# A fused attention and phase-MLP kernel: a fixed order of instructions in place of a scheduler, with gated loads, another way for one batch's transposes, and zero products in TensorE's gaps

## The chip, the cores and the metric

The kernel runs on one core of one Trainium2 chip. The metric is the device time of one execution in microseconds (us). All inputs lie in HBM as float32; q, k, v and the weights are turned into bf16 while they are loaded, and the output is float32.

Names used below: TensorE (PE in the profile; PEld is its weight load), VectorE (DVE), ScalarE (ACT), GpSimd (POOL), SyncE (SP). "Software loads" are DMAs that POOL issues; "hardware loads" are DMAs that SP or ACT issue.

## The reference

Four batches of 768 positions go through sparse attention (8 heads of 64), then through a layer that mixes positions and channels. Cut to what matters:

```python
# attention: keep the first 8 keys and a band of 96 keys behind each query
scores = (q @ k^T) / sqrt(64) - slope[h] * dist(i, j)     # masked where not kept
x = softmax(scores) @ v                                    # to (batch, 768, 512)
# the second layer
theta = x @ w_theta
y = w_tok_r @ (x * cos(theta)) + w_tok_i @ (x * sin(theta))   # mixes the 768 positions
u = x + y
out = u + relu(u @ w_ch)
```

Within a batch everything before the mixing is local to a third of the positions (256). The mixing needs x of the whole batch. So each batch passes through scores, exponentials, values, transposes of x, theta, cosine and sine, mix, u, transposes of u, and the channel product. Other batches' work can fill TensorE while one batch waits.

## The kernel before

The kernel builds a list of named operations with guessed durations, then a list scheduler in Python chooses at build time, greedily by earliest start, the order in which they are written out. Each engine then gets its own instructions in that order, and one that has to wait holds up those behind it.

```python
class Plan:
    LAT = 0.2
    ...
    def schedule(self):
        ...
        while ready:
            best = None
            for o in ready:
                for e, dur in o.eng.items():
                    ...
                    s = max(t, free.get(e, 0.0))
                    key = (s if len(o.eng) == 1 else s + dur * 0.0, o.prio)
                    if best is None or key < best[0]:
                        best = (key, o, e, s, dur)
        ...
        return sorted(order, key=lambda o: o.start)
```

All loads are issued by POOL, one after the other; the code sets no limit on how many are under way. The trace shows one all the same: the loads take turns at eight semaphores that tell of their landing, never more than eight were under way at once, and 26 were issued within 0.45 us of the landing of the load eight places before. There are 80 loads; most bring 128 positions of q, k or v (128 KB once they are bf16):

```python
def load(fn, nbytes, ndesc, reads=(), writes=(), alloc=None):
    nload[0] += 1
    add(f"load{nload[0]}", {"POOL": 0.62 + 0.00028 * ndesc}, fn, ...,
        after=[f"load{nload[0] - 1}"] if nload[0] > 1 else [])
```

From batch 1 on, two small jobs are done by hardware DMAs on SP's queue, beside the loads: the copy of v whose first 8 rows are the global keys (vp), and the transposes of x (and of u):

```python
def vprev(b, g, prio):
    ...
    if b == 0:
        ...   # two copies on DVE
    else:
        add(f"vpa{b}{g}", {"SP": 0.5}, lambda: nc.sync.dma_start(out=dst[NG:T], in_=src[NG:T]), ...)
        add(f"vpb{b}{g}", {"SP": 0.5}, ...)          # the first 8 rows, by DMA too

def xtrans(b, g, prio):
    if b == 0:
        ...   # eight transposes on TensorE, then an evacuation by DVE or ACT
    else:
        add(f"xt{b}{g}", {"SP": 0.5},
            lambda: nc.sync.dma_start_transpose(out=new(xt, "xT", [T, NP, 2, T], BF)..., in_=tiles[xk]...), ...)
```

The keys are kept twice, side by side (one copy gets the global keys). One instruction reads the transposed k from PSUM and writes both copies:

```python
kk = new(dst, "kk", [T, NP, 2, 2, T], BF)
vector[o.took](out=kk.rearrange("d p t r n -> d (p t) r n"),
               in_=tiles[ps].rearrange(...)[:, :, None, :].to_broadcast([T, 2 * NP, 2, T]))
```

PSUM is cut into two tiles of two banks ("big": scores, theta, values in pairs) and four of one bank ("small"). Before its first data arrive TensorE runs eight products of zeros.

The softmax here doesn't subtract the row's maximum and nothing guards it: scores larger than these inputs give would overflow.

## Time and profile before

| | before |
|---|---|
| median time, us | 202.90 (4 runs, 202.41 to 203.18) |
| span of the profiled run, us | 200.8 |
| busy: PE, DVE, ACT, POOL, us | 168.4, 124.7, 92.4, 69.4 |
| granted TensorE clock, mean over the span | 0.937 |
| first theta product, us | 29.12 |
| TensorE waiting for xT, us | 16.7 |

The page cuts the span into 40 slices; each digit is the busy share in tenths, and the PEclk row is the granted clock in tenths. The view of windows gives, for a stretch, the busy time of PE, PEld, DVE, ACT and POOL with the number of instructions in brackets, then the clock, the DMA share and GB/s. The list of waits gives who waited for what: microseconds in all, times, and the longest. The lines of these views are in the prediction below.

```profile
67.52 1.52 SPq L481 DMA_TRANSPOSE xT<-x  x1
...
81.70 0.87 SPq L373 DMA_DIRECT2D vp<-vn  x1
...
83.53 1.51 SPq L481 DMA_TRANSPOSE xT<-x  x1
```

SP stood for 80.5 us in all in front of copies of v whose v had not landed, and what was to be sent later waited behind them. This is a good part of the hole. The x of batch 1's second third was ready at 69.6 us, but in the scheduler's order two copies of batch 2's v come before its transpose; their v landed at 72.65 and 81.64 us, so the transpose left SP at 83.53, 13.9 us late, and landed at 92.99. The transpose of the first third (x ready at 62.5 us) had left at 67.52 and landed at 77.21: 5.1 us in SP's queue and 9.7 in transit.

### The profile page before, as it was taken

To read this page: it belongs to the slowest core of one execution; us is meant where nothing else is said; L and a number is where in the kernel's file an instruction comes from. 1 tells how busy PE (TensorE), PEld (TensorE's weight loads), DVE (VectorE), ACT (ScalarE), POOL (GpSimd) and SP (SyncE) were. 2 spreads that over 40 slices of the span, in tenths; PEclk is the share of its full clock that TensorE was granted. 3 is DMA by queue.
4 is the path that set the end of the run, shared out by engine and by line. 5 is a ranking of instruction groups with operands and counts; after the bars stand their busy time and mean duration, and the time that the engine had idled before them with its cause. 6 is when DMAs were issued, how large, how long until landed. Compare 5 with 4: busy or idle time off the path is not lost.

```text
span 200.8 us, 3765 instructions
## 1 busy us (share of the span) xinstructions
PE 168.4 (84%) x1532; PEld 88.5 (44%) x1532; DVE 124.7 (62%) x243; ACT 92.4 (46%) x100; POOL 69.4 (35%) x85
## 2 busy tenths in 40 slices
PE   7589999899589906804999799999999998999982
PEld 2355466555245502401364355547454653444430
DVE  5475994958496920700397788677988775634351
ACT  2038758899355400600487464187764609400010
POOL 7999745479686855720072000000000000000000
PEclk9859999999999975965899999999999999999998
DMA  5999999999999999999799442832114466124432
GB/s 37 133 147 152 187 210 208 176 154 161 152 184 182 185 138 199 145 148 201 118 102 169 91 131 66 177 100 65 54 30 106 103 148 116 52 52 140 126 104 104
DMA packets 101224, 26.37 MB, mean 131 GB/s; under 512 B 94351, under 2 KB 97055, under 8 KB 101207
## 3 DMA queue, kind: packets, MB, share of 16 engines
q0 software_dynamic: 77568, 12.85, 90.5%
q1 hardware_dynamic: 23639, 13.28, 28.9%
q8 instruction: 12, 0.20, 0.4%
q14 instruction: 5, 0.04, 0.1%
HBM read 25.69 MB, written 6.29 MB: 159 GB/s over the span
## 4 chain that ended last, share of the span: by engine, by line
PE 47%; DMA 33%; POOL 10%; DVE 4%; issue 2%; ACT 1%; SPq 1%; POOLq 0%
PE ps L534 24%; DMA qk<-in_k_dram 11%; PE ps L573 8%; DMA xT<-x 7%; POOL qk L256 6%; PE pb L492 5%; DMA w_nat<-in_moe_w_tok_i_dram 5%; DMA vn<-in_v_dram 5%; DMA out_dram<-o 4%; POOL vn L269 4%; PE pb L448 3%; PE pb L401 3%; DMA uT<-u 2%; PE ps L338 2%; DVE kk L348 1%
## 5 line engine op out<-in xcount | busy, mean ns | idle before, releaser
L534 PE MATMUL ps<-zri,w_tokT 128*128 128x512 bf16 x288 | 70.3, 381 | 0.4 <-ACT w_tokT L327 0.4
L418 ACT ACTIVATE e<-pb 128x1024 bf16<-128x1024 f32 (+1 forms) x48 | 43.9, 951 | 36.3 <-PE pb L401 36.0
L492 PE MATMUL pb<-w_theta_bf,xT 128*128 128x512 bf16 x96 | 25.7, 416 | 16.7 <-DMA xT<-x 16.7
L534 PEld LDWEIGHTS <-w_tokT 128*128 128x128 bf16 x288 | 26.2, 98 | 28.7 <-issue 1.4
L545 DVE TENSOR_TENSOR u<-x,ps 128x512 bf16<-128x512 bf16 x24 | 16.4, 685 | 32.3 <-PE ps L534 32.2
L256 POOL DMA_DIRECT2D qk<-in_q_dram x24 | 21.3, 894 | 25.7 <-PE ps L338 14.7
L426 DVE TENSOR_TENSOR e<-e,etab 128x1024 bf16<-128x1024 bf16 (+1 forms) x36 | 23.0, 642 | 6.7 <-ACT e L418 6.4
L573 PE MATMUL ps<-w_ch_bf,uT 128*128 128x512 bf16 x96 | 24.7, 379 | 1.8 <-DMA uT<-u 1.1
L256 POOL DMA_DIRECT2D qk<-in_k_dram x24 | 21.2, 892 | 5.7 <-DMA qk<-in_q_dram 2.3
L269 POOL DMA_DIRECT2D vn<-in_v_dram x24 | 21.2, 907 | 5.5 <-DMA qk<-in_k_dram 2.0
L492 PEld LDWEIGHTS <-xT 128*128 128x128 bf16 x96 | 9.5, 105 | 30.1 <-DMA xT<-x 18.3
L580 DVE SCALAR_TENSOR_TENSOR o<-ps,u 128x512 f32<-128x512 f32 x24 | 16.6, 690 | 10.0 <-PE ps L573 9.8
L505 ACT ACTIVATE cs<-pb,halfpi 128x1024 bf16<-128x1024 f32 x12 | 13.4, 1114 | 17.5 <-PE pb L492 17.4
L513 DVE TENSOR_TENSOR zri<-x,cs 128x1024 bf16<-128x1024 bf16 x24 | 16.3, 686 | 5.3 <-ACT cs L505 4.8
L338 PE MATMUL ps<-ident,qk 128*128 128x128 bf16 x192 | 15.6, 230 | 4.7 <-DMA qk<-in_q_dram 2.4
L348 DVE COPY kk<-ps 128x2048 bf16<-128x2048 bf16 x12 | 14.5, 1220 | 4.9 <-PE ps L338 4.9
L401 PE MATMUL pb<-qT,kk 64*128 64x128 bf16 x352 | 17.0, 223 | 0.4 <-DVE rec L460 0.4
L401 PEld LDWEIGHTS <-kk 64*128 64x128 bf16 x352 | 10.2, 96 | 14.4 <-issue 12.0
L338 PEld LDWEIGHTS <-qk 128*128 128x128 bf16 x192 | 12.4, 102 | 8.7 <-DMA qk<-in_q_dram 3.4
L505 ACT ACT_TABLE_LOAD x4 | 5.1, 1283 | 23.5 <-PE pb L492 23.5
L448 PEld LDWEIGHTS <-e 128*128 128x128 bf16 x352 | 13.3, 97 | 5.2 <-issue 1.4
L573 PEld LDWEIGHTS <-uT 128*128 128x128 bf16 x96 | 8.5, 98 | 10.8 <-DMA uT<-u 1.7
(53 smaller groups left out, 146.7 us busy)
## 6 DMA issues: line engine op xcount, KB each, us to landing
out_dram<-o SPq DMA_DIRECT2D x24, 256.0 KB, 2.3
qk<-in_q_dram POOLq DMA_DIRECT2D x24, 128.0 KB, 8.3
qk<-in_k_dram POOLq DMA_DIRECT2D x24, 128.0 KB, 8.3
vn<-in_v_dram POOLq DMA_DIRECT2D x24, 128.0 KB, 8.4
vp<-vn SPq DMA_DIRECT2D x9, 243.8 KB, 8.2
w_nat<-in_moe_w_tok_r_dram POOLq DMA_DIRECT2D x3, 384.0 KB, 11.0
w_nat<-in_moe_w_tok_i_dram POOLq DMA_DIRECT2D x3, 384.0 KB, 11.7
w_theta_bf<-in_moe_w_theta_dram POOLq DMA_DIRECT2D x1, 512.0 KB, 6.9
```

Source lines behind the costliest of these rows:

```text
L256: nc.gpsimd.dma_start(out=tiles["qk", b, g][:, i, t].rearrange("p (h d) -> p h d", d=D), in_=(q, k)[i][b, :, r0:r0 + T, :].rearrange("h p ...
L269: nc.gpsimd.dma_start(out=v_bufs[i][:, t, :, 0:D], in_=v[b, :, r0:r0 + T, :].rearrange("h p d -> p h d"))
L338: nc.tensor.transpose(p_[:, p, t * T:(t + 1) * T], src[:, i, t, p * T:(p + 1) * T], ident)
L401: nc.tensor.matmul(p_[:, hh, s * T:(s + 1) * T], lhsT=tiles["kk", b, kg][R, p, kt, r, :], rhs=tiles["qT", b, g][R, p, qt * T:(qt + 1) * T] ...
L418: nc.scalar.activation(e_[:, :, 0:n], tiles[pb][:, :, 0:n * T].rearrange("p a (s n) -> p a s n", n=T), AF.Exp, scale=scale)
L426: nc.vector.tensor_mul(e_[:, :, 0:n], e_[:, :, 0:n], etab[:, 2 * p:2 * p + 2, s0:s0 + n])
L448: nc.tensor.matmul(o, lhsT=l_, rhs=r_, start=(i == 0), stop=(i == len(mms) - 1))
L492: nc.tensor.matmul(p_[:, t, :], lhsT=tiles["xT", b, g][:, p, t, :], rhs=w_theta_bf[:, p, :], start=(p == 0), stop=(p == NP - 1))
L505: nc.scalar.activation(c_[:, 0], tiles[pb], AF.Sin, bias=halfpi)
L534: nc.tensor.matmul(p_, lhsT=w_tokT[wi][:, 2 * g + t, tt * T:(tt + 1) * T], rhs=tiles["z", b, g][:, wi, t, :], start=(g == 0 and t == 0 and ...
L573: nc.tensor.matmul(p_, lhsT=tiles["uT", b, tt][:, p, :], rhs=w_ch_bf[:, p, :], start=(p == 0), stop=(p == NP - 1))
L580: nc.vector.scalar_tensor_tensor(o_, in0=tiles[ps], scalar=0.0, in1=tiles[uk], op0=ALU.max, op1=ALU.add)
```

## The change

The scheduler is taken out, and a list of some 940 names fixes the order. A name may carry the engine that does it ("/DVE") and a number of zero products to put ahead of it ("+27"). With it come changes of method. In the words of the change's title: gated loads; the first third of q and k by hardware loads; the second copy of k from SBUF; zero products in TensorE's gaps; forced table loads. In the diff there is more: x of batch 1 is transposed on TensorE, all vp copies are on DVE, all PSUM tiles are of one bank, and the loads come in another order (the token weights in twelve loads rather than six, between the others). The core of the diff, with cuts:

```diff
-    def schedule(self):
-        ...
+    def issue(self, order):
+        for n in order:
+            n, _, pad = n.partition("+")
+            n, _, eng = n.partition("/")
+            op = self.ops[n]
+            op.took, self.pad = eng or op.took, int(pad or 0)
+            op.fn()
+
+ORDER = """
+ones6 hw00 hw10 zero rel ones3 tiny hw01 halfpi hw11 warm0 ... t0001+27 load8 cast11/DVE ...
+... gate20 x0210 xc01/DVE bi0221+1 load20 v020 x0211 s022 n020 tw00 gate21 ... ch351 o35 st34 o351 st35 st351
+"""
-    bufs = dict(qk=5, ..., cs=2, ..., w_nat=6, big=2, small=4)
+    bufs = dict(qk=6, ..., cs=3, ..., w_nat=7, pa=4, pb=4)      # pa, pb: one PSUM bank each
+    def fill(p_, acc=False):
+        for _ in range(plan.pad):
+            ...  nc.tensor.matmul(p_, lhsT=zero[:, 0:T], rhs=zero[:, 0:p_.shape[-1]], start=not acc, stop=not acc)
-    NV = 6
+    NV = 7
+    VP_ENG = (1, 1, 1, 1)     # copies of v on DVE in all batches
+    X_PE = (1, 1, 0, 0)       # x transposed on TensorE in batches 0 and 1
+    U_PE = (1, 0, 0, 0)
+    DEPTH = 5
+    DP = 80                   # v padded from 65 to 80 columns a head
     ...
+        if depth:
+            add(f"gate{n}", {"POOL": 0.35},
+                lambda: nc.gpsimd.tensor_copy(out=scrap, in_=landed[n - depth]()),   # reads one element of load n-5
+                reads=[("ld", n - depth)], ...)
     ...
+    def first(i, t):          # first q/k third: float32 by hardware load, then a cast
+            (nc.sync, nc.scalar)[i].dma_start(out=a, in_=(q, k)[i][0, :, t * T:(t + 1) * T, :]...)
     ...
+            def copy():       # second copy of k: from SBUF
+                vector[oc.took](out=d_[:, :, :, 1, NG:T], in_=d_[:, :, :, 0, NG:T])
     ...
+            add(f"tx{b}", {"ACT": 1.36}, lambda: nc.scalar.activation(tiny, tiny, AF.Exp), ...)
+        add(f"ts{b}", {"ACT": 1.36}, lambda: nc.scalar.activation(tiny, tiny, AF.Sin), ...)
```

A gate is a POOL copy of a single element that load number n-5 has brought; as POOL works in order, load n is not issued before load n-5 has landed (for every load from 20 on, the first that is gated). So the gates bring loads under way down to five. A forced table load is an activation of one element that makes ScalarE load the table of Exp or Sin at a moment when it is free.

## The prediction

> **What bounds the kernel now.** I read the page first (engine shares, the 40 slices), then the windows cut at the points where the character of the 40 slices changes, then the waits of TensorE, the timeline of TensorE in the worst stretch, and the two tiles that travel by hardware DMA.
>
> The page, shares and slices:
>
> ```profile
> PE 168.4 (84%) x1532; PEld 88.5 (44%) x1532; DVE 124.7 (62%) x243; ACT 92.4 (46%) x100; POOL 69.4 (35%) x85
> ...
> PE   7589999899589906804999799999999998999982
> ...
> PEclk9859999999999975965899999999999999999998
> DMA  5999999999999999999799442832114466124432
> ```
>
> TensorE is the bound from slice 20 on (9s to the end), but slices 13 to 19 hold a hole with the clock down to 5 or 6 tenths, and the first slices are half empty. Each slice is 5.02 us. The DMA row is 9 for the first 19 slices and falls to 1 to 6 afterwards: the hole in TensorE ends where the load queue runs dry. The same, by stretches:
>
> ```profile
> 7.00:29.00 22.00, 19.55 (x267) 12.04 (x265) 15.86 (x39) 11.47 (x13) 18.29 (x24) 0.84 1.89 168
> 29.00:60.00 31.00, 26.67 (x266) 15.98 (x265) 22.25 (x41) 23.56 (x30) 21.34 (x25) 1.00 2.09 174
> 60.00:69.80 9.80, 9.80 (x132) 5.37 (x129) 7.67 (x16) 5.46 (x6) 7.25 (x10) 1.00 2.14 182
> 69.80:101.90 32.10, 15.94 (x94) 7.22 (x91) 9.09 (x17) 7.12 (x7) 11.76 (x14) 0.73 1.82 158
> 101.90:162.00 60.10, 58.50 (x603) 31.20 (x602) 47.96 (x85) 35.59 (x38) 4.85 (x6) 1.00 0.55 99
> ```
>
> After the window and its length come PE, weight loads, DVE, ACT and POOL busy, the granted clock, DMA share and GB/s. From 69.80 to 101.90 only 94 matmuls ran in 32.10 us, at a mean clock of 0.73; the next 60.10 us ran 603 at 58.50 busy. What TensorE waited for:
>
> ```profile
> PE pb L492 <- DMA xT<-x: 16.7, 4, 8.4
> PE ps L338 <- DMA qk<-in_q_dram: 2.4, 3, 1.5
> PE ps L338 <- DMA qk<-in_k_dram: 1.7, 4, 0.6
> PE pb L393 <- DVE dtab L232: 1.6, 1, 1.6
> ```
>
> L492 is the theta product; it waits for the attention output of batch 1, transposed by a hardware DMA. Its timeline lines, and the landing times of the two tiles that go by DMA transpose:
>
> ```profile
> 77.26 3.20 PE L492 MATMUL pb<-w_theta_bf,xT 128*128 128x512 bf16 x8 [7.29 <-DMA xT<-x]
> 93.04 3.59 PE L492 MATMUL pb<-w_theta_bf,xT 128*128 128x512 bf16 x8 [8.42 <-DMA xT<-x]
> 98.18 1.90 PE L492 MATMUL pb<-w_theta_bf,xT 128*128 128x512 bf16 x8 [0.45 <-DMA xT<-x]
> ```
> ```profile
> DMA to landing us min/median/max: 3.2/8.5/9.7
> ```
> ```profile
> DMA to landing us min/median/max: 2.4/2.4/2.9
> ```
>
> The first is xT, whose transposes of batch 1 were issued into the loads; the second is uT, used by DMA only after 107 us, when few loads run. So a transpose costs 3 us alone and 8 to 10 behind the loads. The second wait is longer than one transpose because the copy of v (vp) stood ahead of it: it landed after a median of 8.2 us, and values and the next transpose waited in turn. The eight matmuls after each hole took 3.20 and 3.59 us instead of 1.90: the clock had dropped.
>
> **What the Trainium skill says.** (1) "TensorE: Matmul & The Clock Gate", Part 1, says that the array starts at half clock and is throttled again after an idle window of about 3.4 us. The trace agrees: holes of 7.29 and 8.42 us, then 3.20 and 3.59 us for work that takes 1.73 to 1.90 elsewhere. (2) "DMA: Bandwidth & Descriptors", section on issuing engines not being separate DMA queues, says that DMAs of all issuers share the 16 engines and interleave. The trace agrees: 8.5 us for xT beside loads against 3.2. (3) "ScalarE: Activation LUTs", section on the cost of a table load, gives about 1283 ns; the trace has 1283 ns for each of its eight. (4) "VectorE: DVE Perf Modes", the walkthrough of the modes, says that a one-source bf16 copy within SBUF can use both read ports and four elements a cycle, and a PSUM source cannot. The trace agrees: the double k copy from PSUM, 128x2048, takes 1.22 us, while the 128x1040 SBUF copy of v takes 0.53.
>
> **The change part by part.** I count TensorE's work with the rates of this trace: a 512-column product 0.216 us (four in 0.86), a transpose 0.056 (sixteen in 0.90 before the tail), a score group 0.37 to 0.43 with its switch (8 products 0.33, and the next wide group 0.11 longer), a value group 0.20 to 0.25 per head pair (16 products 0.48). The old kernel: mix 288, theta 96 and channel 96 products are 480 x 0.216 = 103.7; scores 48 groups 18.7; values 48 groups 11.2; 316 transposes 17.7; 24 bias products 4.8; the warm-up 3.6. Sum 159.7. Checked on the stretch 102 to 160 us: 180 wide products 38.9, 22 score groups 9, 144 value products 4.5, 80 transposes 4.5, sum 56.9 against 56.4 measured. So of the 200.8 us some 41 are start, holes, cold clock and tail.
>
> Removed: (a) The hole. Work of 69.8 to 101.9 at full clock: 48 wide products 10.4, 8 and 16 transposes 1.35, 16 values 0.5, together 12.2 of 32.1 us, so 19.9 us lost (16.2 idle, the rest cold clock). The change moves batch 1's x transposes to TensorE (24 x 0.056 = 1.35 us added), makes the vp copies of batches 1 to 3 on DVE (18 copies of some 0.55, +9.9 us of DVE), and lets at most five loads be in flight: the transposes of u that go by DMA in batch 1 then queue behind five loads of about 0.9 us, not ten. Net gain 18.5 if nothing takes its place. (b) The start. Theta begins at 29.1. The trace's landing records show software loads landing 0.87 us apart, first at 4.8, the last of the first q/k third at 8.8, the last v of batch 0 at 22.4. Four loads leave that queue for SP and ACT, whose issue needs no 0.9 us of POOL each; the first third should land by 6 to 7, v near 19.5 to 20. DVE has 22.4 us of work before the first theta by my count from the order of the changed kernel (setup 5.7, casts, evacuations, vp, norms), ACT 17.1 (with the etab exponentials moved ahead of the scores, where it was idle), TensorE 19.5. DVE starts near 1 us, so theta begins near 24: gain 5. (c) Between 39 and 60 us TensorE waited 4.3 us (q/k loads, w copies, u). A depth of five must not make that worse; I take 2.5 as gained. (d) Later: waits of 1.1 and 0.5 plus table loads at the head of cos, now forced earlier; 1.5. (e) The tail: the last channel product is halved, its output store with it; 0.5.
>
> Added: 63 zero products stand in the order where TensorE was expected to wait; they cost only where the wait is shorter, some 0.5. The k copy within SBUF saves about 0.3 us x 12 of DVE and ACT; single value groups in place of pairs add some 4.5 of DVE. DVE comes to 136, ACT to 102: neither reaches TensorE's sum in any stretch after theta (between the first scores of batch 1 and its theta: 29.5 TensorE, 24.7 DVE, 19.6 ACT).
>
> Sum from above: 200.8 - 18.5 - 5 - 2.5 - 1.5 - 0.5 + 0.5 = 173.3. Sum from below: theta at 24, then 162.0 - 19.5 = 142.5 of TensorE, 2.5 of waits, 3.7 of tail: 172.7. I take a span of 172.7; the measured time has been 1.8 over the span (202.59 and 200.8), so 174.5.
>
> **The rivals.** First, POOL becomes the bound of loading. Each gated load is 0.88 us of issue plus a small POOL copy that reads what landed; I estimate that at 0.35 from the 0.38 us of its iota, so 1.25 us per load in place of 0.87 to 0.9. From the twentieth load near 22 us, load 82 would issue near 98. For batch 3, needed from about 110, that is early; for batch 1 it is tight: q/k of its third 1 are loads 31 to 34, landing near 39 to 42, and TensorE wants them near 41 to 46. If the copy costs 0.6, TensorE waits some 5 us between 30 and 60 us, and the time is 180. For it: POOL's slices are 6 to 9 already. Against it: the weight loads issue faster.
>
> Second, DVE becomes the bound in batch 1, where it gets the vp copies, singles, and multiplications, in strict order: if the copies of 65 of 80 columns run at a slower mode (1.2 us rather than 0.53), DVE gains 13 us in all, 3 or 4 per batch, and the time is 177 to 178. The window 101.9 to 162 shows DVE 80% busy beside a full TensorE, so the slack is real but not large.
>
> Third, a fixed order is brittle: an instruction of TensorE placed ahead of a late operand blocks all behind it. Each such miss is 0.5 to 1 us; ten of them give 180. Fourth, the hole was the load bandwidth and not the queue ahead of the transposes; then only its place would move, and the time would be 185 to 190. Against it: from 69.8 TensorE waited for xT, not for q or k of batch 2, which landed by then.
>
> **Range and chances.** The two sums agree near 173 of span; the rivals add 3 to 8 each and are not exclusive; a better start or fewer waits take off 3 or 4. So 174.5, with 169.5 to 182 for eight in ten. Slower than 199 would need the whole gain of the hole to vanish: faster 0.97, within 2% 0.02, slower 0.01.
>
> **What would show it.** Right: no TensorE wait for xT over 1 us before 100 us; clock 1.0 in that stretch; theta's first product between 23 and 25.5; uT landing in 3 to 5 us during loads; DVE near 136, ACT near 102 busy; POOL near 90 to 100. Wrong: waits of TensorE for qk or w_nat between 30 and 60 over 4 us in sum (first rival); DVE full with TensorE waiting for x, e or kk (second); many short waits scattered over the whole run (third); a new hole on the loads of batch 2 (fourth).

## More of the kernel before

From the waits of SP and from its timeline in the kernel before:

```profile
SPq L373 <- DMA vn<-in_v_dram: 80.5, 9, 44.2
```

## The result, and the profile after

The changed kernel took 173.77 us (median of 4 runs, 172.58 to 174.35) against 202.90. The ratio is 0.856, with a 95% interval of 0.850 to 0.861. Ratios here are the mean time of one kernel's runs over that of the other's runs of the same rounds, so not quite the ratio of the medians. Executions over 1.5% slower than the fastest of the same kernel are left out of the means. The result is correct.

From the page of the changed kernel, busy times and three rows of slices (a slice is now 4.3 us):

```profile
PE 162.9 (94%) x1598; PEld 93.2 (54%) x1623; DVE 133.4 (77%) x315; ACT 106.0 (61%) x187; POOL 85.0 (49%) x150
...
PE   7998999999997999999999997999999999999991
...
PEclk9999999999999999999999999999999999999999
DMA  5999999999999999999999999612335364134334
```

PE's row has no hole any more, and the clock is full in every slice. The DMA row is full for the first 25 slices, to some 108 us, where it had been full for the first 22 of 5.0 us, to some 110. The last load lands at 107.1 us; before it landed at 111.9. So the DMA engines are as busy with loads as before, for nearly as long, and TensorE has stopped waiting for what passes through them.

The stretch of the hole, by the view of windows:

```profile
69.80:101.90 32.10, 31.60 (x342) 18.21 (x347) 31.36 (x76) 25.19 (x45) 28.78 (x50) 1.00 2.11 144
```

From 69.8 to 101.9 us TensorE was busy for 31.60 us where it had been busy for 15.94, at a clock of 1.00 instead of 0.73. DVE is at 31.36 of 32.10: it is as full as TensorE there, and yet TensorE has no long wait for it. What TensorE still waits for:

```profile
PE pb L341 <- DVE zero L181: 1.2, 1, 1.2
PE pa L549 <- DMA xT<-x: 1.1, 1, 1.1
PE pb L371 <- DMA qk<-in_k_dram: 1.0, 1, 1.0
```

The first is the start of the program. The second is the theta product of batch 2, at 106.5 us, whose x still goes by DMA; the third comes at 56.1 us, and an experiment below asks whose it is. The first theta product stands in TensorE's timeline at

```profile
27.04 1.04 PE L549 MATMUL pa<-w_theta_bf,xT 128*128 128x512 bf16 x4
```

against 29.12 before. The forced table load for Sin in ScalarE's timeline:

```profile
27.69 0.59 ACT L474 ACTIVATE e<-pa 128x512 bf16<-128x512 f32 x1
28.30 1.28 ACT L673 ACT_TABLE_LOAD   x1
29.59 0.20 ACT L673 ACTIVATE tiny<-tiny 1x1 f32<-1x1 f32 x1
29.70 0.77 ACT L358 COPY w_tokT<-pb 128x768 bf16<-128x768 bf16 x1
```

The table is loaded between the last exponential and a plain copy, while the theta products that need it are still running. Last, three groups of new instructions, from the groups of instructions by shape (count, busy us, mean ns):

```profile
L230 POOL COPY scrap<-qk 1x1 bf16<-1x1 bf16 x33 | 11.3, 343 | 5.1 <-DMA qk<-in_k_dram 2.6 <-DMA qk<-in_q_dram 2.3
L409 DVE COPY vp<-vn 128x1040 bf16<-128x1040 bf16 x12 | 6.1, 510 | 0.0
L391 DVE COPY kk<-kk 128x960 bf16<-128x960 bf16 x10 | 4.7, 470 | 1.3 <-ACT kk L380 1.2
```

A gate's record is some 0.34 us long (0.22 on v). It delays the next load by less: loads 20 to 23 are issued 1.0 us apart, and ungated ones 0.87. The v copy takes 0.51 us in all batches, against 0.53 before, so the padding to 80 columns did not slow it down. The k copy within SBUF takes 0.47 us.

Where the 28.2 us of span went, by four marks in TensorE's timelines (each batch has 88 score products). The marks are places in an order that is not the same in both kernels, so they say the stage, not the cause:

| stretch | before, us | after, us | gained, us |
|---|---|---|---|
| start to first theta product | 29.12 | 27.04 | 2.1 |
| to the first score product of batch 1 | 17.10 | 12.24 | 4.9 |
| to the first of batch 2 (batch 1's attention and mixing) | 60.62 | 40.86 | 19.8 |
| to the first of batch 3 | 36.23 | 36.88 | -0.6 |
| to the end | 57.73 | 55.58 | 2.1 |

### The profile page after: what moved, and what is told of

It is laid out like the page before. It is cut to its first block, busy times and chain, and to the rows that moved or that the text cites. A ratio compares the mean times of both kernels' runs of the same rounds, so it can differ in the third digit from the quotient of the medians.

```text
span 172.6 us, 4153 instructions
## 1 busy us (share of the span) xinstructions
PE 162.9 (94%) x1598; PEld 93.2 (54%) x1623; DVE 133.4 (77%) x315; ACT 106.0 (61%) x187; POOL 85.0 (49%) x150
## 4 chain that ended last, share of the span: by engine, by line
PE 48%; DMA 30%; POOL 6%; DVE 6%; issue 5%; ACT 2%; DVEq 0%; POOLq 0%; SPq 0%; ACTq 0%
PE pb L592 22%; DMA qk<-in_k_dram 10%; PE pb L636 9%; PE pa L549 8%; DMA w_theta_bf<-in_moe_w_theta_dram 5%; DMA qk<-in_q_dram 4%; DMA xT<-x 4%; DMA uT<-u 3%; POOL qk L243 3%; DMA w_ch_bf<-in_moe_w_ch_dram 3%; PE pa L451 3%; PE pa L504 3%; PE pb L371 2%; POOL scrap L230 1%; DVE e L482 1%
## 5 line engine op out<-in xcount | busy, mean ns | idle before, releaser
L592 PE MATMUL pb<-zri,w_tokT 128*128 128x512 bf16 x273 | 67.3, 379 | 1.1 <-issue 0.5
L474 ACT ACTIVATE e<-pa 128x512 bf16<-128x512 f32 (+1 forms) x96 | 46.5, 565 | 20.0 <-PE pa L451 19.4
L592 PEld LDWEIGHTS <-w_tokT 128*128 128x128 bf16 x288 | 26.1, 98 | 28.2
L604 DVE TENSOR_TENSOR u<-x,pb 128x512 bf16<-128x512 bf16 x24 | 16.4, 682 | 11.9 <-PE pb L592 11.7
L636 PE MATMUL pb<-w_ch_bf,uT 128*128 128x512 bf16 (+1 forms) x96 | 24.0, 370 | 0.3
L549 PE MATMUL pa<-w_theta_bf,xT 128*128 128x512 bf16 x93 | 22.5, 379 | 1.3 <-DMA xT<-x 1.1
L482 DVE TENSOR_TENSOR e<-e,etab 128x1024 bf16<-128x1024 bf16 (+1 forms) x36 | 22.4, 639 | 0.4
L558 ACT ACTIVATE cs<-pa,halfpi 128x512 bf16<-128x512 f32 x24 | 16.6, 693 | 9.4 <-PE pa L549 9.2
L642 DVE SCALAR_TENSOR_TENSOR o<-pb,u 128x512 f32<-128x512 f32 (+1 forms) x25 | 16.2, 663 | 3.7 <-PE pb L636 3.7
L517 DVE TENSOR_TENSOR x<-pa,rec 128x256 bf16<-128x256 f32 x36 | 15.3, 425 | 1.2
L620 ACT COPY uT<-pb 128x512 bf16<-128x512 bf16 x4 | 2.4, 594 | 20.9 <-PE pb L616 20.9
L451 PE MATMUL pa<-qT,kk 64*128 64x128 bf16 x352 | 14.9, 218 | 0.0
L560 ACT ACTIVATE cs<-pa 128x512 bf16<-128x512 f32 x24 | 14.4, 602 | 0.0
```

The source lines that it names most:

```text
L451: nc.tensor.matmul(p_[hh][:, s], lhsT=tiles["kk", b, kg][R, kt, p, r, :], rhs=tiles["qT", b, g][R, qt, p, :], start=not biased, stop=not b ...
L474: nc.scalar.activation(tiles[ek][:, hh, 0:n], tiles[pb[hh]][:, 0:n], AF.Exp, scale=scale)
L482: nc.vector.tensor_mul(e_[:, :, 0:n], e_[:, :, 0:n], etab[:, 2 * p:2 * p + 2, s0:s0 + n])
L549: nc.tensor.matmul(p_, lhsT=tiles["xT", b, g][:, p, t, :], rhs=w_theta_bf[:, p, :], start=(p == 0), stop=(p == NP - 1))
L558: nc.scalar.activation(tiles[ck][:, 0], tiles[ps], AF.Sin, bias=halfpi)
L592: nc.tensor.matmul(p_, lhsT=w_tokT[wi][:, 2 * g + t, tt * T:(tt + 1) * T], rhs=tiles["z", b, g][:, t, wi, :], start=(n == 1 and t == 0 and ...
```

## The experiments

Two theories stood at the start. Mine: the hole was a matter of small jobs that travelled through the DMA engines during the loads, so taking them off is most of the gain, and the gates are a help at most. The rivals: the gates, by keeping the queue short, are what removed the hole; or the fixed order did it, or other parts of the change. Kernels called "after with ..." are the changed kernel with one part undone; "before with ..." are the kernel before with one part done alone. Lines of code in the changed kernel move by a line or two in them. Two limits hold for all: a kernel "after with ..." keeps an order that was made for the changed kernel, and in a kernel "before with ..." the scheduler makes a new order for all engines. All twelve gave correct results. The numbers of all:

| run | what it is | median us (runs) | ratio to before | 95% |
|---|---|---|---|---|
| a_xdma | after, x of batch 1 by DMA | 183.88 (4) | 0.908 | 0.901 to 0.914 |
| a_vpdma | after, v copies by DMA, long fills at the start | 182.59 (4) | 0.901 | 0.894 to 0.908 |
| a_nogate | after, no gates | 172.91 (4) | 0.854 | 0.848 to 0.859 |
| a_all3 | after, all three | 189.08 (4) | 0.934 | 0.928 to 0.940 |
| b_xvp | before, x of batch 1 on TensorE, v copies on DVE | 192.64 (4) | 0.948 | 0.940 to 0.955 |
| b_gate | before, gates | 192.85 (4) | 0.950 | 0.943 to 0.958 |
| a_lategate | after, gates only from load 47 | 172.12 (4) | 0.850 | 0.843 to 0.858 |
| a_control | after, unchanged | 174.63 (6) | 0.859 | 0.853 to 0.864 |
| a_nopads | after, no zero products in the order | 172.38 (6) | 0.849 | 0.845 to 0.854 |
| a_swfirst | after, first q/k third by software loads | 175.15 (6) | 0.859 | 0.852 to 0.867 |
| a_kpsum | after, second k copy from PSUM | 175.73 (6) | 0.864 | 0.858 to 0.869 |
| a_vpdma2 | after, v copies by DMA, fills moved | 182.12 (4) | 0.897 | 0.887 to 0.907 |

The first four shared a chip and the runs of the kernel before (median 202.07); so did the next three (202.93), and the four from a_control to a_kpsum (203.18); a_vpdma2 ran by itself (202.39).

### a_xdma: is it the road of batch 1's x?

```diff
-    X_PE = (1, 1, 0, 0)
+    X_PE = (1, 0, 0, 0)
```

The evacuations that then have no operation are left out of the order.

> The changed kernel with one part undone: batch 1's attention output is transposed by DMA again, its three evacuations dropped, gates and v copies on VectorE kept. Theory (the transposes of batch 1 had to leave the DMA engines while loads run): xT lands 5 to 6 us after issue instead of 8.5, and TensorE waits some 2.5 us for the first theta and 5 us for the next ones: 179 to 184 us. Rival (a queue of at most five loads is what removes the hole): under 177 us and no wait for xT over 2 us.

Measured 183.88 us. The profile is of a run that was slow (185.81 us against 183.01 to 184.18 of the other three), so I read only where it waits. TensorE's timeline:

```profile
74.11 1.89 PE L550 MATMUL pa<-w_theta_bf,xT 128*128 128x512 bf16 x4 [5.63 <-DMA xT<-x]
...
84.99 2.57 PE L550 MATMUL pa<-w_theta_bf,xT 128*128 128x512 bf16 x8 [3.64 <-DMA xT<-x]
```

The waits for xT are back: 5.63 us, and then four products that take 1.89 us instead of 0.87, because the clock has fallen. Gates were on, at most five loads were under way, and still the three transposes landed 9.2, 9.3 and 6.1 us after the start of their issue; in the kernel before it was 9.7, 9.5 and 8.5. The time came as the theory said, but not its 5 to 6 us of landing. The road of x is worth some 10 us in this order, and a queue of five does not make DMA transposes fast enough. Part of the 10 us is the order's: the x of the first third was ready at 52.6 us, and its transpose stands where TensorE was to do it, so it was issued at 64.87. A DMA transpose placed early was not tried.

### a_vpdma: do the v copies on DVE matter?

```diff
-    VP_ENG = (1, 1, 1, 1)
+    VP_ENG = (1, 0, 0, 0)
...
-            lambda i=i: nc.vector.memset(v_bufs[i][:, :, :, D:D + 1], 1.0), ...
+            lambda i=i: nc.vector.memset(v_bufs[i][:, :, :, D:DP], 1.0), ...
```

A DMA copies whole rows, so the columns 65 to 80 must be written first.

> The changed kernel with the copies of v for batches 1 to 3 back on SP's DMA. Theory: v lands 8 us before it is used in batch 1, so a DMA copy of 5 to 6 us still arrives in time for most thirds: 174 to 178 us, VectorE busy 9 us less. Rival (the v copies ahead of the transposes made the hole): 182 us or more, with TensorE waiting for vp.

Measured 182.59 us: above the expected range. The experiment had a fault of its own. The wider fills took 0.27 us each instead of 0.07 and stood at the head of DVE's order; the first score product came at 12.90 us instead of 10.02. So up to 2.9 us of the loss is the experiment's doing. The rival's 182 us came true, but TensorE waits for xT and uT (2.9 and 2.1 us), not for vp. It is repeated below as a_vpdma2.

### a_nogate: are the gates the cure?

```diff
-        if depth:
+        if False:
```

> The changed kernel without the POOL copies that hold a load until the fifth before it has landed. Theory: with xT of batch 1 and the v copies off the DMA engines only the u transposes of batch 1 and the stores stand behind loads; they take 8 us instead of 5 and most is hidden by the order: 173 to 178 us, and the wait for the k of batch 1's last third (0.97 us at 56 us) goes. Rival (the gates are the main part): 185 us or more.

Measured 172.91 us (171.75 to 173.22), within the noise of the changed kernel's own 172.58 to 174.35 and if anything faster. The hole does not come back. With x and v off the DMA engines the gates buy nothing in time. The first transpose of u landed in 7.6 us here against 5.4 in the changed kernel, and TensorE waited for it for 0.7 us. But without gates the last load lands at 88.6 us instead of 107.1, so everything after it finds free DMA engines: the next five transposes of u took 2.4 to 3.3 us (with gates 3.3 to 6.0), the three of batch 2's x 3.0 to 3.2 (with gates 6.7 to 7.3). So in this kernel the gates stretch the loads by 18.5 us and make most DMA transposes slower. The rival "the gates did it" falls, for this kernel.

### a_all3: all three undone

The edits of a_xdma, a_vpdma (with its fault: the first score product comes at 11.51 us) and a_nogate together.

> The changed kernel with all three undone: x transposes of batch 1 and v copies by DMA, no gates; fixed order, hardware loads, k copy, zero products and table loads kept. Theory: the hole comes back between 65 and 100 us, 15 to 20 us of TensorE's waits for xT, 188 to 195 us. Rival (the fixed order makes the gain): under 180 us.

Measured 189.08 us, in the range; TensorE's waits for xT are 11.4 us, under the 15 to 20 of the theory. TensorE's timeline:

```profile
74.51 1.89 PE L550 MATMUL pa<-w_theta_bf,xT 128*128 128x512 bf16 x4 [5.73 <-DMA xT<-x]
...
86.64 3.60 PE L550 MATMUL pa<-w_theta_bf,xT 128*128 128x512 bf16 x8 [5.33 <-DMA xT<-x]
```

This looks much like the lines before: two holes over 5 us and cold products after them. Yet it is still 13 us better than the kernel before (ratio 0.934). That remainder belongs to what was not undone: the order, the one-bank PSUM tiles, the start, the order of the loads, and the rest of the change; no run divides it.

### b_xvp: the two moves alone, in the kernel before

```diff
 def vprev(b, g, prio):
-        if b == 0:
+        if True:
 def xtrans(b, g, prio):
-        if b == 0:
+        if b <= 1:
```

The old scheduler makes a new order, with the new DVE and TensorE work where it sees fit.

> The kernel before with one idea of the change alone: batch 1's x transposes on TensorE and all v copies on VectorE; its own scheduler, its load queue and everything else kept. Theory (these two made the hole): 183 to 190 us, with no wait for xT of batch 1 over 1 us, clock 1.0 from 60 to 100 us. Rival (the fixed order or the gates make the gain): 197 us or more.

Measured 192.64 us: a miss, by 2 to 9 us. No wait for xT is left among TensorE's longer ones; others stand in their place. First TensorE's waits, then DVE's:

```profile
PE ps L573 <- DVE uT L560: 3.3, 2, 2.8
PE ps L556 <- DVE u L545: 3.2, 2, 2.4
```
```profile
DVE vp L367 <- DMA vn<-in_v_dram: 9.3, 6, 4.9
```

The v copy is now in DVE's strict order. The scheduler guessed when v would land, v landed later, and DVE stood in front of the copy for up to 4.9 us with u and uT behind it, which TensorE needed. So the move of the copies is good only together with an order that puts them late enough. This is the first part of the answer to where the order's worth lies.

### b_gate: the gates, in the kernel before

```diff
+        if n >= 20:
+            add(f"gate{n}", {"POOL": 0.35},
+                lambda: nc.gpsimd.tensor_copy(out=scrap, in_=landed[n - 5]()), reads=[("ld", n - 5)], ...)
```

> The kernel before with gates alone (from the twentieth load on, each waits until the fifth before it has landed). Theory: xT lands in 5 to 6 us instead of 8.5, v copies likewise; of the chain copy, values, transpose, three times, some 3 us each are saved, but loads go at POOL's 1.1 us pace: 190 to 198 us. Rival (the short queue is the main part): 185 us or less.

Measured 192.85 us: in the range, and as large a gain as b_xvp's. xT's landing times (least, median, longest; of the two landings that are in the trace), and TensorE's waits:

```profile
DMA to landing us min/median/max: 6.8/7.2/7.5
```
```profile
PE ps L583 <- DMA uT<-u: 5.3, 4, 2.7
PE pb L502 <- DMA xT<-x: 3.0, 1, 3.0
```

A transpose of x still needs 7.2 us instead of 8.5, and yet TensorE's wait for xT falls from 16.7 us to 3.0. The landings alone can't do that; SP's queue does. Batch 1's transposes leave SP at 56.22, 65.23 and 73.13 us, each within 0.2 us of the moment when its x is ready; in the kernel before they left 5.1, 13.9 and 6.7 us late. For this edit is not the gates alone: the scheduler counts the gates' time, plans the loads later, and now puts each transpose of batch 1 ahead of the copies of batch 2's v. What the gates would do in the old order was not tried. So in the old kernel this edit is worth about 10 us, and in the new one the gates are worth nothing. It and the moved transposes are two cures of the same hole, not two parts of a sum. One row of 60 to 100 us for each of four kernels (before, b_xvp, b_gate, the changed kernel) shows it:

```profile
60.00:100.00 40.00, 23.84 (x198) 11.16 (x196) 15.23 (x29) 10.80 (x11) 18.61 (x22) 0.79 1.97 166
```
```profile
60.00:100.00 40.00, 30.43 (x304) 16.86 (x304) 29.35 (x56) 18.70 (x20) 21.61 (x25) 0.91 1.61 124
```
```profile
60.00:100.00 40.00, 33.29 (x335) 17.75 (x339) 28.06 (x51) 21.61 (x24) 30.30 (x58) 0.96 2.02 175
```
```profile
60.00:100.00 40.00, 39.40 (x450) 22.97 (x455) 38.74 (x94) 32.02 (x57) 37.06 (x65) 1.00 2.03 141
```

TensorE's busy time goes 23.84, 30.43, 33.29, 39.40 of 40.00, with clocks of 0.79, 0.91, 0.96, 1.00. Each cure alone fills part of the hole; only the changed kernel fills it.

### a_lategate: who waits for k at 56 us?

The gates begin at load 47, so that the loads of batch 1 (up to load 46) run free.

```diff
-        if depth:
+        if depth and n > 46:
```

> The changed kernel with gates only from load 47 on (batches 2 and 3), free before. Theory: until 56 us nothing but stores shares the DMA engines, so the gates only slow POOL there (1.1 us a load against 0.87); the wait of 0.97 us for k at 56 us goes: 0.5 to 1.5 us faster than the changed kernel, 172 to 173.5 us. Rival (the free loads delay stores and their buffers): same or slower.

Measured 172.12 us (171.86 to 173.32), as expected. Its trace has no wait for k at 56 us. The last k of batch 1 (load 42) lands at 48.6 us; in the changed kernel it lands at 56.1, and TensorE waits for it there for 1.0 us. So the gates do slow the early loads, as the first rival of the prediction had it: a load and its gate take POOL 1.0 us even where the gate does not wait, more than the 0.87 us at which loads land, and five under way are fewer than eight. The loss is 1 us in the trace, and too small to be seen for certain in the times: 0.8496 against 0.8559, with intervals that overlap.

### a_control, a_nopads, a_swfirst, a_kpsum: four small parts, five rounds each

a_control is the changed kernel once more, to have it on the same chip in the same rounds as the next three.

> The changed kernel itself again, as the control for the small effects of this call: 172.5 to 174.5 us.

Measured 174.63 us (173.56 to 174.87, 6 runs).

a_nopads takes the 63 zero products out of the order (the eight at the start stay). Of the 63, 50 are transposes of a tile of zeros and 13 are plain products:

```diff
-            op.took, self.pad = eng or op.took, int(pad or 0)
+            op.took, self.pad = eng or op.took, 0
```

> The changed kernel without its 63 zero products. Theory: they keep the granted clock at 1.0 through the start (the kernel before had 0.75 between 10 and 20 us); without them the clock falls below 0.9 somewhere between 5 and 25 us and the first theta comes 1 to 2 us later: 174 to 176 us. Rival (they only fill waits whose end something else sets): within 0.5 us of the control.

Measured 172.38 us (171.71 to 173.09, 6 runs). None of its runs is as slow as the fastest of a_control. Both theories missed: the clock fell as the first had it, but the kernel becomes 2.2 us faster, where one expected it slower and the other expected no difference. Windows of a_control, then of a_nopads:

```profile
7.00:27.00 20.00, 18.95 (x293) 13.43 (x294) 15.35 (x44) 14.83 (x28) 13.50 (x21) 1.00 1.95 165
27.00:60.00 33.00, 30.77 (x309) 18.63 (x314) 25.81 (x55) 22.58 (x41) 25.98 (x53) 1.00 1.51 150
```
```profile
7.00:27.00 20.00, 16.52 (x242) 11.18 (x244) 15.51 (x44) 14.82 (x28) 13.99 (x21) 0.91 2.04 165
27.00:60.00 33.00, 32.63 (x355) 20.47 (x362) 27.54 (x60) 24.87 (x44) 28.45 (x56) 1.00 1.64 163
```

The zero products do what they are for: with them the clock is 1.00 from 7 to 27 us, without them 0.91. The transposes among them do it too: from 7 to 10 us all but three of a_control's 45 products are transposes, and its clock there is 1.00. Cut finer, a_nopads shows when it falls:

```profile
7.00:10.00 3.00, 1.11 (x16) 0.67 (x18) 2.80 (x9) 2.29 (x4) 2.79 (x4) 0.96 2.42 155
10.00:13.00 3.00, 2.75 (x24) 2.06 (x24) 0.86 (x2) 1.64 (x4) 2.96 (x4) 0.50 2.44 154
```

TensorE was busy for 1.11 us of the three from 7 to 10, and in the next three it ran at half clock. In the Trainium skill, "TensorE: Matmul & The Clock Gate", section on HAM oscillation, gives the rule as no idle gap above some 3.4 us. Here no single gap was longer than 1.56 us, and the clock fell all the same; so the measurement is stricter than the rule. What the traces show is a share and not a gap. In all 14 the granted clock changes only on a grid of 3.41 us; in a_nopads it is full from 6.32 to 9.73 us and half from there to 13.15. TensorE's busy share, worked out from the matmul records for each of the 683 grid windows at full clock, tells what follows: the 20 that were busy for at most 0.44 of their length were all followed by half clock, the 661 above 0.47 all by full clock, and of the two between one by each. In a_nopads the window from 6.32 us was busy for 0.41; in the kernel before, those that opened the two cold stretches of the hole (69.69 and 83.34 us) for 0.08 and 0.37.

But the first theta product comes at 26.90 us with the zero products and at 26.95 without, so the higher clock gains nothing in the end. At 22.4 us the kernel with zero products is 0.27 us ahead (the same value products begin at 22.39 and at 22.66), and it loses that to two later sets of zero products, at 23.28 and 24.36 us. The gain of leaving them out comes later, from 27 to 60 us, where TensorE does 1.9 us more. There the loads land sooner: the last k of batch 1 lands at 54.7 us instead of 57.4, and the waits for k, 1.6 us in a_control, are gone.

How zero products can delay loads is argued and not shown. Instructions too are fetched by DMA: the trace has twelve transfers of 16 KB on an instruction queue, which I take for TensorE's, as leaving out its products shifts them. In the changed kernel one fetch begins at 14.8 us and takes 1.4 us, and the load that was to land then comes 2.38 us after the one before (15.71 to 18.09 us) instead of 0.9; in a_nopads the first fetch comes at 20.1 us and those two loads land 0.90 us apart. In a_control a second pause stands beside the third fetch: it begins at 30.17 us and takes 2.45, and the loads around it land at 30.79 and 33.96. Zero products are instructions, so they bring the fetches forward into the loads. No run changes the fetches alone.

a_swfirst loads the first third of q and k by POOL, cast in flight, as before:

```diff
-            first(i, t)
+            sw_first(i, t)          # nc.gpsimd.dma_start into the bf16 tile; the cast on DVE is dropped
```

The first names of the order are also changed a little (the iota of POOL comes first).

> The changed kernel with the first q/k third loaded by POOL with the cast in the DMA, as before; the four VectorE casts go. Theory (the hardware loads bring the start forward): the first third lands 0.7 to 1 us later, as in the kernel before (8.8 us), so first scores come 0.5 to 1 us later: 0.5 to 1.5 us slower than the control. Rival (both ways share the same DMA engines and the casts cost VectorE what the loads gain): within 0.5 us of the control, or faster.

Measured 175.15 us (173.43 to 176.97, 6 runs, two of them slow), ratio 0.859 like the control's. The first score product came at 9.96 us against 10.01, the first theta product at 27.58 against 26.90, and the four loads landed by 8.16 us against 8.28. The rival was right: the hardware loads gain nothing that can be measured at the end; the 0.7 us at theta do not reach it.

a_kpsum takes the second copy of k from PSUM again, right after the first:

```diff
-                vector[oc.took](out=d_[:, :, :, 1, NG:T], in_=d_[:, :, :, 0, NG:T])
+                vector[oc.took](out=d_[:, :, :, 1, NG:T], in_=tiles[ps][:, :, :, NG:T])
```

> The changed kernel with the second k copy read from PSUM again, straight after the first. Theory: each such copy of 128x960 takes some 0.65 us on VectorE instead of 0.45, in all 2 us of VectorE, and holds its PSUM buffer that much longer; VectorE is not the bound after the start: 0 to 1 us slower than the control. Rival (VectorE or the PSUM buffers are at their limit): 2 us or more slower.

Measured 175.73 us (173.80 to 176.03, 6 runs), 1.1 us above the control, with ratios whose intervals overlap (0.864 against 0.859). The group of this copy:

```profile
L394 DVE COPY kk<-pb 128x960 bf16<-128x960 bf16 x10 | 6.5, 652 | 2.4 <-ACT kk L383 2.4
```

It takes 652 ns from PSUM against 470 in the changed kernel. Ten copies make 1.8 us of DVE, of which at most 1.1 reach the end.

### a_vpdma2: the v copies by DMA, without the fault

As a_vpdma, but the columns 65 to 80 are written by separate fills, placed in the order where DVE is free:

```diff
-... s000+3 kp001/DVE load10 ...
+... s000+3 kp001/DVE pad3 pad4 pad5 pad6 load10 ...
-... vpb10/DVE z020 mx011 ...
+... vpb10/DVE z020 pad0 pad1 pad2 mx011 ...
```

> As a_vpdma, but with a cleaner edit: in a_vpdma wider memsets at the very start moved the first scores from 10.0 to 12.9 us. Here the unused columns that the DMA reads are set later, in gaps of VectorE at 11 and 33 us. Theory: the 3 us of the start come back, the waits near 98 us (u behind loads) and 117 us (xT of batch 2, later loads) of 2 to 3 us each stay, since v copies queue on SP before them: 177 to 179.5 us. Rival (the v copies by DMA cost nothing of their own, the first edit did it all): under 175 us.

Measured 182.12 us (180.42 to 183.19, one of four runs slow). A miss again: the theta product now starts at 27.62 us, near the changed kernel's 27.04, and still 8 us are lost. The v copies by DMA cost that by themselves, in this order. SP's waits:

```profile
SPq L422 <- DMA vn<-in_v_dram: 53.4, 9, 34.4
```

SP's queue stands for 53.4 us in front of copies that wait for v, as in the kernel before (80.5). The last x of batch 2 was ready at 102.6 us, and its transpose left SP only at 106.05, behind a copy of v that landed at 105.03. And the last two loads of the program land at 113.6 and 115.4 us instead of 106.2 and 107.1; that the copies take room on the DMA engines from the loads is the likely reason, but not shown. The theta product that needs that x waits 2.92 us until 115.2, and the first score product of batch 3 comes at 124.79 us instead of 117.02, so the whole loss of 7.6 us of span is there by then.

## Why the prediction was right, point by point

The time was predicted at 174.5 us and measured at 173.77; the span at 172.7, and measured at 172.6. That is closer than the parts deserve, and in so far luck: two of them were wrong by some 3 us in opposite directions.

**The hole (18.5 us): right in size.** Between the first score products of batches 1 and 2 the changed kernel is 19.8 us quicker, no wait for xT stands before 100 us, and the clock is 1.00, as the checks of the prediction asked. Its reason was the road of x and v: a_xdma loses 10 us and a_vpdma2 8 us against the changed kernel. Two readings under it were off. The second wait was put down to the time that a copy of v takes to land; the trace has the transpose standing in SP's queue for 13.9 us behind copies of the next batch's v. And the hole was said to end "where the load queue runs dry": the DMA row is at 9 again in the two slices after the 7, and loads landed until 111.9 us; in between POOL had waited 14.7 us for a buffer of q and k that TensorE had to free. The part that rested on five loads in flight, the transposes of u that "then queue behind five loads of about 0.9 us, not ten", came out neither in its numbers nor in its worth: eight loads were under way and not ten, uT landed 4.9 to 6.0 us after the start of its issue while loads ran (predicted 3 to 5), and a_nogate loses nothing.

**The start (5 us): the step that failed.** The first theta product came at 27.04 us, not 24. The prediction let "four loads leave that queue for SP and ACT", so that "the first third should land by 6 to 7". They landed at 4.75, 5.43, 7.47 and 8.07 us, and the software loads before at 4.78, 6.33, 7.93 and 8.79: moving the issue to other engines did not make room on the DMA engines, which all loads share. That is what the prediction itself quotes in its second point from the Trainium skill, and its own step on the start did not apply it. The last v of batch 0 landed at 20.9 us (expected 19.5 to 20), and w_theta, which I had not put on the path at all, at 23.4. a_swfirst confirms it: no difference in time. "DVE starts near 1 us, so theta begins near 24" also took it that DVE would work without a break: it was busy for 21.2 us of the 27.04, near the 22.4 counted, and idle for 5.8. From a_nopads, the gaps of TensorE lie before 16 us, where it waits for casts, copies and the v copy, which wait for loads; from 16 to 27 us it is busy for 10.83 of 11. So loads bound the first part of the start, and TensorE's own work the rest.

**TensorE's work after theta: over-priced by about as much.** Predicted: 142.5 us of work and 2.5 of waits, 145.0. Measured from the first theta product to the end of the last product: 168.76 - 27.04 = 141.7 us, waits included. The likely term is the scores: I charged 0.37 to 0.43 us for eight products, and in this trace eight are followed by the next group after 0.33 us and sixteen after 0.55. With 36 such groups after theta, 0.1 us each is an estimate of 3.6 us. No run separates this term.

**Waits between 39 and 60 us (2.5 us) and later (1.5 us).** From the first theta product to the first score product of batch 1 4.9 us were gained, from the first of batch 3 to the end 2.1. They are the right size together with the start: 5 + 2.5 was predicted for everything up to the first score product of batch 1, and 6.9 was measured. The tail's 0.5 did not come: from the end of the last product to the end of the span it was 3.9 us before (196.9 to 200.8) and 3.8 after.

**Zero products (0.5 us): too low.** They cost about 2 us (a_nopads). The sum from below starts from 162.0 us of TensorE work, which the prediction does not derive.

**The rivals.** The first, POOL as the bound of loading, is real but small: 1.0 to 1.6 us of waits for k, gone in a_lategate and a_nogate. My estimate of 0.35 us for a gate fits its record of 0.22 to 0.34, but a load with a gate that need not wait took 1.0 us of POOL and not 1.25; POOL was busy for 85.0 us, not 90 to 100. The second, DVE in a slow mode, did not occur: 510 ns for the v copy. (The pair of copies in the prediction's fourth point from the Trainium skill does not carry it: 1.22 us for 2048 columns and 0.53 for 1040 are 0.60 and 0.51 ns a column. The pair of a_kpsum does: 652 ns from PSUM and 470 within SBUF for the same 960 columns.) DVE's 133.4 us and ACT's 106.0 stand beside 136 and 102 expected. The third, brittleness, did not occur in the changed kernel, but b_xvp shows what it looks like when an order does not fit the landings. The fourth, bandwidth as such, is excluded: with loads about as dense as before and ending 4.8 us sooner, the hole of 20 us is gone, and no new one stands on batch 2's loads; in a_nogate the loads end at 88.6 us, so there had been room.

**What stays open.** The parts do not add up, as several cure the same hole. From b_xvp (192.6) to the changed kernel (173.8) there are some 19 us that belong to the fixed order, the one-bank PSUM tiles, the order of the loads and the gates together; a_all3 shows some 13 us of this kind. No run takes the order alone or the PSUM tiles alone, since the order names operations that only exist with the new tiles. One obvious rival cure was not tried either: the old kernel with nothing changed but SP's order, each transpose of batch 1 ahead of the copies of batch 2's v. What the forced table loads are worth was not tried by a run; the trace shows only that they stand where ScalarE is free. a_nopads (172.38) and a_lategate (172.12) are both slightly better than the changed kernel; both together were not run.

## What to carry to other kernels

While the DMA engines are full of loads, take small transfers that something waits for off them (a transpose onto TensorE, a copy onto VectorE), because each took 7 to 10 us there and a fraction of one on an engine; look at the queue that sends them too, since a transpose that is ready can stand for 13.9 us behind a copy that is not; but put them late enough in a strictly ordered engine that they do not wait for their own load. Undo each part of a large change by itself and do it by itself: the two results differ where parts cure the same wait (and where a scheduler makes a new order for the part), and here the gates and the zero products turned out to be of no use in the kernel that contains them. Before you price a shorter start, ask which resource the first data are waiting for: another engine to issue the loads does not help when the transfers share the same DMA engines.

## What the Trainium skill lacked or had wrong

- "DMA: Bandwidth & Descriptors", section on latency and other measured facts, gives 600 ns to the first byte for hardware loads and about 1 us for software loads. It has no case of a burst at the start, where that difference did not show: the last of the four first loads landed at 8.28 us by hardware (a_control) and at 8.16 by software (a_swfirst), and the kernels took 174.63 and 175.15 us.
- The same page, section "DMA Transpose (X-bar)", has constraints but no landing time of one transpose beside other traffic. From the start of the issue: 2.4 to 3.4 us in the changed kernel once the loads had landed, 8.5 to 9.7 beside up to eight loads in the kernel before, 4.9 to 7.3 beside up to five in the changed kernel, and up to 9.3 so in a_xdma.
- "Runtime: NRT & Kernel Launch", section "Instruction fetch mechanics", calls the cost of crossing a 16 KiB block "mostly hidden". Here such fetches took 0.9 to 2.5 us each during the loads, and beside one of them the landing of loads paused for 2.38 us instead of 0.9. That one causes the other was not shown.
- "ScalarE: Activation LUTs", section "What ACT_TABLE_LOAD costs", adds a drain of about 1380 ns to the 1283 ns of a table load. In this trace a forced load began 0.02 us after the exponential before it ended and the next activation began 1.29 us after the load began: no drain shows. The other six forced loads show the same two gaps of under 0.02 us.
- "TensorE: Matmul & The Clock Gate", section on HAM oscillation, warns of idle gaps above some 3.4 us, and the section after it of frequent short ones, without a figure. In a_nopads the clock fell to 0.50 with no gap above 1.56 us. In the 14 traces the busy share of a window of 3.41 us decided: at most 0.44, and half clock followed; above 0.47, full clock. The page has no such share, and no price for filling gaps with products of zeros: 63 of them held the clock at 1.00 instead of 0.91 for 20 us, and the kernel was 2.2 us slower with them.
- "GPSIMD Engine Reference" has no time for a copy of one element, the means of gating a queue: 219 to 343 ns here.
